# Logits of two of five blocks formed in four column ranges, from bfloat16 pieces

## The chip, the cores and the metric

The kernel runs on one core of one Trainium2 chip. The metric is the time of one execution on the device in microseconds (us). Three runs of the kernel before took 920.73, 920.84 and 923.83 us; their median is 920.84 us.

## The reference, cut to what matters

Three layers follow each other: a linear attention with random features, a gated feed-forward layer, and a layer of eight experts whose routing is greedy and global. The change touches the second layer's hidden rows `h` and the logits of the third.

```python
# x: (2304, 512), from the attention
xn = x / rms * rms_g
g = xn @ w_gate                      # (2304, 1536)
val = xn @ w_val
h = g * (1.0 / (1.0 + np.exp(-g))) * val
y = h @ w_out                        # (2304, 512)
logits = y @ w_gate2                 # (2304, 8)
# tokens are given to experts by the sorted logits, 288 to each of the 8
for e in range(8):
    out[mask_e] = np.maximum(y[mask_e] @ w1[e], 0.0) @ w2[e]
```

The routing orders all 2304 x 8 logits against each other, so the logits need more accuracy than one pass of short numbers gives.

## The kernel before, in words

**Blocks and half-steps.** The 2304 tokens are cut into five blocks `j` = 0 to 4, four of 512 tokens and a last one of 256 (`WIDTH`). The 1536 hidden features are cut into twelve slices `f` of 128. A half-step `(j, f, v)` is the gate product (`v` = 0) or the value product (`v` = 1) of one slice of one block: `ffn_pe` (L652) issues 12 matmuls into a PSUM tile `gv`: four times L659 and L660 (high and low part of the weights against the high part `xh` of the tokens), then four times L662 (high weights, low part `xl`). Every operand is float32r, split into a high and a low part. `ffn_el` (L665) works on the result: for `v` = 0 a tanh on ACT (L671) and a product on DVE (L672), for `v` = 1 the product with the gate on DVE (L684), the high part on ACT (L686), the low part on POOL (L687) and a store of both to DRAM (`h_dr`, L688).

**Logits.** Since `logits = h @ (w_out @ w_gate2)`, they are formed from `h` directly: `wog` holds, for each slice, the 8 columns of `w_out @ w_gate2` as a high and a low part, 16 columns in all. `ffn_lg` (L691) multiplies them with the high part (L698) and the low part (L699) of one slice of one block: two float32r matmuls of 16 weight columns and as many moving columns as the block has tokens, summed over the 12 slices in a PSUM tile `lg`. `ffn_rank` (L705) transposes the sums (L710), adds the halves (L712, L713) and `ranks` (L97 to L101) counts within each token.

**Block 0 comes late.** When block 0 runs, `wog` isn't ready. Its `h` is stored unsplit (L680, L682), and behind the attention a loop reads it back slice by slice (`late_load`, L894), splits it (`late_split`: L899 on ACT, L900 on POOL), writes the parts to DRAM (L901) and forms its logits in a PSUM tile `late`.

**Stages.** From 0 to about 390 us the attention runs in ticks, with half-steps of the blocks between its matmuls. Then comes the loop that begins at `late_load(0)`: 45 half-steps, the rest of block 3 and all of block 4. It is called the tail here. From about 500 us `w_out` is applied to all tokens (`ffn2`, L972) as filler between the matmuls of the routing (`route`; its counting products are L181), and from about 685 us the experts run.

**What sets the order.** In the ticks and in the routing the order of TensorE (PE) is the order in which the code is written. In the tail of the kernel before, a scheduler orders every engine, PE too; on the other engines it may also move work of the tail in front of work of the ticks. Each engine, and the queue of SP that issues nearly all DMAs, works strictly in its order. Tiles come from pools with a fixed number of buffers: `gv` has 2, `ht` 6 (`HB`), `ws` 3 (pool `stage`), `dw` 3, `hp` 2, `th` 2. `wo_split` (L871) loads two slices of `w_out` and splits them, on ACT (L876) and DVE (L877).

Of the kernel before, what the change touches and what calls it, by code (L numbers as in the profile page):

```python
# [9 lines left out]
F32 = mybir.dt.float32  # L10
F32R = mybir.dt.float32r
# [3 lines left out]
OP = mybir.AluOpType  # L15
# [88 lines left out]
def route(nc, keep, sb, ps, cst, L, R, ids, slot, aside, room):  # L104
# [10 lines left out]
    for n in (NSL, SL, 2 * NSL):  # L115
# [176 lines left out]
def kernel(ctx, tc, qT, kT, kC, v1, vC, om, wgv, rms, wo, woT, wg2, w1, w2, cfd, trd, cid, out, dbg=None):  # L292
# [356 lines left out]


    fq, fst, lgs, rks = [], {}, [], []

    def ffn_pe(j, f, v):
        n = WIDTH[j]
        pg = psG.tile([128, BLK], F32, name="gv")
        w = wsl[f].rearrange("p l (v k m) -> p l v k m", k=KD, v=2)
        xh, xl = xblk[j]
        for k in range(KD):
            nc.tensor.matmul(pg[:, :n], w[:, 0, v, k], xh[:, k, :n], start=(k == 0), stop=False)  # L659
            nc.tensor.matmul(pg[:, :n], w[:, 1, v, k], xh[:, k, :n], start=False, stop=False)  # L660
        for k in range(KD):
            nc.tensor.matmul(pg[:, :n], w[:, 0, v, k], xl[:, k, :n], start=False, stop=(k == KD - 1))  # L662
        return pg[:, :n]

    def ffn_el(j, f, v, pg):  # L665
        n = WIDTH[j]
        nh = n // HB2
# [21 lines left out]
        fq.append((j, f, hp))  # L689

    def ffn_lg(j, f, hp):  # L691
        n = WIDTH[j]
        nh = n // HB2
        if f == 0:
            st["lg", j] = (psL if j else psB).tile([2 * E, BLK], F32, name="lg" if j else "late", bufs=1)
        wv = wog[:, f].rearrange("p a e -> p (a e)")
        lg = st["lg", j][:, :n].rearrange("p (b t) -> p b t", b=nh)
        nc.tensor.matmul(lg, wv, hp[:, :nh, 0], start=(f == 0), stop=False)  # L698
        nc.tensor.matmul(lg, wv, hp[:, :nh, 1], start=False, stop=(f == KF - 1))  # L699
        if f == KF - 1:  # L700
# [24 lines left out]
    def ffn_step_pe():  # L725
# [116 lines left out]
    with tc.manual_schedule(engines={mybir.EngineType.PE}):  # L842
# [16 lines left out]
    st["rank"] = lambda: psB.tile([128, 512], F32, name="num", bufs=1)[:, :BLK // 128 * 2 * E].rearrange(  # L859
        "p (c e) -> p c e", e=2 * E)  # L860
# [28 lines left out]
    lates, step = [], 0  # L889

    def late_load(f):
        hs = f2.tile([128, 4, 2, 128], F32R, name="ht", bufs=HB)
        hs = hs.rearrange("p a l t -> p (a l t)").rearrange("p (b l t) -> p b l t", b=BLK // HB2, l=2)
        nc.sync.dma_start(hs.bitcast(F32)[:, :, 1], h_dr[:BLK // HB2, :, f, :HB2].rearrange("b p x -> p b x"))  # L894
        lates.append(hs)

    def late_split(f):
        hs = lates[f]
        nc.scalar.copy(hs[:, :, 0], hs.bitcast(F32)[:, :, 1])  # L899
        nc.gpsimd.tensor_sub(hs[:, :, 1], hs.bitcast(F32)[:, :, 1], hs[:, :, 0])  # L900
        nc.sync.dma_start(h_dr[:BLK // HB2, :, f].rearrange("b p x -> p b x"),  # L901
                          hs.bitcast(F32).rearrange("p b l t -> p b (l t)"))

    late_load(0)
    while True:
        if not ffn_step_pe():
            break
        lf, lv = divmod(step, 2)
        if not lv and 0 < lf <= KF:
            ffn_lg(0, lf - 1, lates[lf - 1])  # L910
        j, f, v = ffn_step_el()
        if lv and lf < KF:
            late_split(lf)
            if lf + 1 < KF:
                late_load(lf + 1)
        if j == NB - 1 and v:
            if f % 2 and f > 1:
                wo_split((f - 3) // 2)
            if f > 6:
                ffn2_load(*seq2[f - 7])  # L920
        step += 1
# [296 lines left out]
```

## Time and profile before

| | |
|---|---|
| median of three runs | 920.84 us |
| the profiled execution, its own time | 922.03 us |
| its span in the trace | 920.2 us |
| granted clock of PE, mean | 0.995 of full speed |
| PE / DVE / ACT / POOL busy | 901.9 / 554.2 / 372.8 / 229.8 us |

The span is the time between the first and the last instruction of the trace; 1.8 us of the execution lie around it. A matmul's row lasts from its start to its modelled end, and matmuls overlap, so the pace of PE is read from the distance between two starts.

### The profile page before, as it was taken

Reading aid. Unit: us, or ns where it says so; the run is one execution under the profiler, and the core shown is the slowest. Engines: PE = TensorE matmul, PEld = TensorE weight load, DVE = VectorE, ACT = ScalarE, POOL = GpSimd, SP = SyncE. Lnnn points to the kernel's source line nnn. Section 1 sums busy time; section 2 is a strip of 40 time slices with the busy share of each in tenths; the row PEclk is TensorE's granted clock in tenths of the full one; section 3 lists DMA queues with packets and bytes.
Section 4 is the critical chain, followed back from the end, with each engine's and each line's share of the span. In section 5 each row is a group of like instructions: output and inputs, shape, how many; then the busy total and the mean of one; then the engine's idle time right before and its main releaser. Section 6 shows DMA issues by size and latency. Waiting matters only on the chain.

```text
span 920.2 us, 16173 instructions
## 1 busy us (share of the span) xinstructions
PE 901.9 (98%) x6171; PEld 783.3 (85%) x6171; DVE 554.2 (60%) x1262; ACT 372.8 (41%) x843; POOL 229.8 (25%) x298
## 2 busy tenths in 40 slices
PE   8998999999999999999999999999999999999996
PEld 7887888888888888877799777777779999999995
DVE  4798896565676775332273666666654655556661
ACT  5985565435554445333252001000014454544541
POOL 1355352122233332275232000000012222122111
PEclk9999999999999999999999999999999999999998
DMA  8556354444345552187564776776623666665550
GB/s 295 182 160 213 120 168 127 135 152 144 115 153 178 184 185 90 69 278 277 189 225 152 202 207 191 211 206 201 171 78 115 193 188 193 189 208 193 184 161 26
DMA packets 113213, 158.88 MB, mean 173 GB/s; under 512 B 6640, under 2 KB 70768, under 8 KB 113136
## 3 DMA queue, kind: packets, MB, share of 16 engines
q1 hardware_dynamic: 107328, 143.57, 49.4%
q0 software_dynamic: 3072, 9.44, 3.4%
q10 hardware_dynamic: 2736, 4.85, 1.4%
q8 instruction: 48, 0.79, 0.3%
q14 instruction: 29, 0.24, 0.1%
HBM read 113.79 MB, written 44.04 MB: 172 GB/s over the span
## 4 chain that ended last, share of the span: by engine, by line
PE 84%; issue 7%; DVE 5%; POOL 2%; DMA 2%; ACT 1%; SPq 0%; POOLq 0%; ACTq 0%; DVEq 0%
PE py L972 16%; PE gv L659 10%; PE gv L660 10%; PE gv L662 10%; PE pm L497 3%; PE ph L1086 3%; PE ph L1083 3%; PE ph L1084 3%; PE py L1094 3%; PE py L1095 3%; PE py L1096 3%; PE pm L440 2%; PE cnt L181 2%; PE pm L486 2%; PE pp L388 1%
## 5 line engine op out<-in xcount | busy, mean ns | idle before, releaser
L659 PE MATMUL gv<-xh,wc 128*128 128x512 f32 (+1 forms) x480 | 180.9, 383 | 2.5 <-DVE th L672 1.9
L660 PE MATMUL gv<-xh,wc 128*128 128x512 f32 (+1 forms) x480 | 175.3, 372 | 0.0
L972 PE MATMUL py<-wc,ht 128*128 128x512 f32 x648 | 167.1, 404 | 0.0
L972 PEld LDWEIGHTS py<-wc,ht 128*128 128x128 f32 x648 | 114.9, 189 | 19.0
L662 PE MATMUL gv<-xl,wc 128*128 128x512 f32 (+1 forms) x480 | 118.4, 369 | 0.0
L659 PEld LDWEIGHTS gv<-xh,wc 128*128 128x128 f32 x480 | 91.1, 190 | 19.5 <-DVE th L672 3.0
L660 PEld LDWEIGHTS gv<-xh,wc 128*128 128x128 f32 x480 | 91.2, 190 | 13.9
L662 PEld LDWEIGHTS gv<-xl,wc 128*128 128x128 f32 x480 | 85.5, 189 | 15.9
L400 ACT ACTIVATE ft<-pp,mx 128x128 f32<-128x128 f32 x288 | 82.3, 372 | 18.5 <-DVE mx L397 16.0
L687 POOL TENSOR_TENSOR hp<-th,hp 128x512 fp32r<-128x512 f32 (+1 forms) x48 | 60.6, 1262 | 114.5 <-ACT hp L686 102.6
L672 DVE SCALAR_TENSOR_TENSOR th<-th,gv 128x512 f32<-128x512 f32 (+1 forms) x60 | 37.9, 632 | 84.4 <-ACT th L671 84.4
L943 DVE TENSOR_TENSOR wc<-ws,wc 128x512 fp32r<-128x512 f32 x128 | 84.8, 683 | 0.0
L1094 PE MATMUL py<-ehh,wc 128*128 128x288 f32 x256 | 77.7, 304 | 0.0
L1095 PE MATMUL py<-ehl,wc 128*128 128x288 f32 x256 | 75.9, 297 | 0.0
L1096 PE MATMUL py<-ehh,wc 128*128 128x288 f32 x256 | 75.8, 296 | 0.0
L1083 PE MATMUL ph<-exh,wc 128*128 128x288 f32 x256 | 71.6, 302 | 0.0
L1084 PE MATMUL ph<-exh,wc 128*128 128x288 f32 x256 | 69.8, 295 | 0.0
L983 ACT COPY ys<-py 128x512 f32<-128x512 f32 x18 | 10.6, 587 | 144.6 <-PE py L972 103.7
L953 ACT CAST wc<-ws 128x1024 fp32r<-128x1024 f32 x64 | 66.9, 1046 | 2.7 <-ACT ys L983 2.4
L397 DVE TENSOR_REDUCE mx<-pp 128x4 f32<-128x512 f32 (+1 forms) x76 | 50.0, 657 | 16.6 <-PE pp L393 10.1
L1088 DVE SCALAR_TENSOR_TENSOR ehl<-ph,ehh 128x288 fp32r<-128x288 f32 x64 | 29.3, 458 | 46.8 <-ACT ehh L1087 46.8
L671 ACT ACTIVATE th<-gv 128x512 f32<-128x512 f32 (+1 forms) x60 | 33.2, 554 | 59.4 <-PE gv L662 52.0
(214 smaller groups left out, 1717.5 us busy)
## 6 DMA issues: line engine op xcount, KB each, us to landing
ws<-in_w_dram SPq DMA_DIRECT2D x64, 512.0 KB, 4.3
ht<-h_dr SPq DMA_DIRECT2D x54, 512.0 KB, 4.1
h_dr<-hp SPq DMA_DIRECT2D x36, 512.0 KB, 2.9
ws<-in_wgv_dram SPq DMA_DIRECT2D x24, 512.0 KB, 4.3
h_dr<-hp SPq DMA_DIRECT2D x24, 256.0 KB, 2.3
ws<-in_woT_dram SPq DMA_DIRECT2D x12, 512.0 KB, 3.6
ws<-in_wo_dram SPq DMA_DIRECT2D x12, 512.0 KB, 3.7
h_dr<-ht SPq DMA_DIRECT2D x12, 512.0 KB, 3.1
```

Source lines behind the costliest of these rows:

```text
L400: nc.scalar.activation(ft[:n, g], pp[:n, g], AF.Exp, bias=mx[:n, g:g + 1])
L659: nc.tensor.matmul(pg[:, :n], w[:, 0, v, k], xh[:, k, :n], start=(k == 0), stop=False)
L660: nc.tensor.matmul(pg[:, :n], w[:, 1, v, k], xh[:, k, :n], start=False, stop=False)
L662: nc.tensor.matmul(pg[:, :n], w[:, 0, v, k], xl[:, k, :n], start=False, stop=(k == KD - 1))
L943: nc.vector.tensor_sub(w[:, 1, h], sv[:, h], w[:, 0, h])
L953: nc.scalar.copy(w[:, 0], sv)
L972: nc.tensor.matmul(py, ht[:, i4, a], w[:, l, f % 2], start=(f == 0 and n == 0), stop=(f == KF - 1 and n == 2))
L1083: nc.tensor.matmul(ph, w[:, 0, k, m], xh[:, k], start=(k == 0), stop=False)
L1084: nc.tensor.matmul(ph, w[:, 1, k, m], xh[:, k], start=False, stop=False)
L1094: nc.tensor.matmul(py, w[:, 0, k], hh[:, k], start=(k == 0), stop=False)
L1095: nc.tensor.matmul(py, w[:, 0, k], hl[:, k], start=False, stop=False)
L1096: nc.tensor.matmul(py, w[:, 1, k], hh[:, k], start=False, stop=(k == KE - 1))
```

## The change

The logits of block 0 and block 3 (the first and the fourth) are formed in another way.

- The weights `wog` are added up to float32 and cut into three bfloat16 pieces: 24 columns of a slice, padded with zeros to 32 (`wb`, in the room of the later tile `ge6`).
- `h` of these blocks is cut into three bfloat16 pieces as well (`split3`: two subtractions on DVE). A piece is the upper or lower half of a float32 word, and is read with a stride of two.
- `group` takes four slices at a time: for each of the three pieces four matmuls, whose outputs lie in partitions 0 to 31, 32 to 63, 64 to 95 and 96 to 127 of a PSUM tile. A slice's place among the four turns from group to group. The sums of both blocks are transposed whole, 128 x 128, and one reduction on DVE adds the 16 parts of each logit.
- The tail's loop is written out anew (`tail`), and PE follows its code. PSUM tiles of half-steps alternate in pairs between `gv` and `py`, two buffers each. The stored rows of block 0 are loaded four ahead. A group stands three half-steps or more behind the half-step that gave its last piece. Loads of `w_out` stand a step ahead of their splits.
- `late_split` writes the high and low part from two `dw` tiles in two DMAs, where one DMA wrote both from `ht`.

```diff
-        nc.vector.scalar_tensor_tensor(th, pg, 0.5, th, op0=OP.mult, op1=OP.mult)
-        h = th.rearrange("p (b t) -> p b t", b=nh)
+        pc = st["pieces"]() if "pieces" in st and j in WIDE else None
+        hs = pc[:, 0] if pc is not None else th
+        nc.vector.scalar_tensor_tensor(hs, pg, 0.5, th, op0=OP.mult, op1=OP.mult)
+        h = hs.rearrange("p (b t) -> p b t", b=nh)
...
+    def split3(pc):
+        h, r = pc[:, 0], pc[:, 1]
+        nc.vector.tensor_sub(r, h, half(h, 1))
+        nc.vector.tensor_sub(half(r, 0), r, half(r, 1))
+
+    def group(four):
+        for n in range(3):
+            for i, (j, f, pc) in enumerate(four):
+                if ("lg", j) not in st:
+                    st["lg", j] = (psL if j else psB).tile([128, BLK], F32, name="lg" if j else "late", bufs=1)
+                src = (half(pc[:, 0], 1), half(pc[:, 1], 1), half(pc[:, 1], 0))[n]
+                nc.tensor.matmul(st["lg", j][32 * i:32 * i + 32, :WIDTH[j]], st["wb"][:, f], src,
+                                 start=(j, i) not in begun, stop=n == 2, skip_group_check=True)
+                begun.add((j, i))
+        for j, f, _ in four:
+            if f == KF - 1:
+                ls = fp.tile([128, BLK], F32, name="th")
+                nc.scalar.copy(ls[:, :WIDTH[j]], st.pop(("lg", j))[:, :WIDTH[j]])
+                wide.append((j, ls))
...
+        for j, ls in wide[:1]:
+            n, c = WIDTH[j] // 128, j * BLK // 128
+            pl = st["rank"]()
+            for i in range(n):
+                nc.tensor.transpose(pl[:, i, :], ls[:, i * 128:(i + 1) * 128], ident)
+            nc.vector.tensor_reduce(out=L[:, c:c + n, :], in_=pl[:, :n].rearrange("p c (g e) -> p c e g", e=E),
+                                    axis=AX.X, op=OP.add)
...
+    def tail():
...
+        step, born, gone, turns, nsplit = 0, [], 0, 0, 0
+        while ffn_step_pe(*(("gv", psG), ("py", psB))[step // 2 % 2]):
+            if step > 2 and born[step - 3] - gone >= 4:
+                four = [pq.pop(0) for _ in range(4)]
+                group(four[turns:] + four[:turns])
+                gone, turns = gone + 4, (turns + 1) % 4
+            j, f, v = ffn_step_el()
+            if v and j in WIDE:
+                split3(pq[-1][2])
+            if nsplit < KF and (step % 2 == 0 or step == 1):
+                late_split(nsplit)
+                nsplit += 1
+            elif step % 2 and len(lates) < KF:
+                late_load(len(lates))
+            if j == NB - 1 and v:
+                if f % 2:
+                    if f > 1:
+                        wo_split((f - 3) // 2)
+                    wo_load(f // 2)
...
     def late_load(f):
-        hs = f2.tile([128, 4, 2, 128], F32R, name="ht", bufs=HB)
...
+        pc = room4() if f % 3 == 2 else stage.tile([128, 2, BLK], F32, name="ws")
...
     def late_split(f):
...
+        pc = lates[f]
+        hi, lo = (fp.tile([128, DM], F32, name="dw", bufs=DW) for _ in range(2))
+        nc.scalar.copy(hi.bitcast(F32R), pc[:, 0])
+        nc.gpsimd.tensor_sub(lo.bitcast(F32R), pc[:, 0], hi.bitcast(F32R))
+        for n, w in enumerate((hi, lo)):
+            nc.sync.dma_start(h_dr[:BLK // HB2, :, f, n * HB2:(n + 1) * HB2].rearrange("b p x -> p b x"),
+                              w.rearrange("p (b x) -> p b x", x=HB2))
+        split3(pc)
+        pq.append((0, f, pc))
...
-        if not lv and 0 < lf <= KF:
-            ffn_lg(0, lf - 1, lates[lf - 1])
...
+    for f in range(4):
+        late_load(f)
+    st["pieces"] = room4
+    with tc.manual_schedule(engines={mybir.EngineType.PE}):
+        tail()
```

PE, first logits of both blocks in the tail (`lg` is block 3, `late` block 0). Before, one slice of each block follows a value product:

```order
L662 MATMUL gv<-xl,wc 128x512 x4
L698 MATMUL lg<-hp,wog 16x512
L699 MATMUL lg<-hp,wog 16x512
L698 MATMUL late<-ht,wog 16x512
L699 MATMUL late<-ht,wog 16x512
L659 MATMUL gv<-xh,wc 128x512
```

Now the first group stands there: two slices of block 3 and two of block 0, in the column ranges 0 to 3.

```order
L666 MATMUL gv_4475<-xl_3174,wc_501 128x512 x4
L714 LDWEIGHTS ge6_4353
L714 MATMUL lg_4488<-ht_4371,ge6_4353 32x512
L714 LDWEIGHTS ge6_4353
L714 MATMUL lg_4488<-ht_4389,ge6_4353 32x512
L714 LDWEIGHTS ge6_4353
L714 MATMUL late_4491<-ws_4361,ge6_4353 32x512
L714 LDWEIGHTS ge6_4353
L714 MATMUL late_4491<-ws_4363,ge6_4353 32x512
L714 LDWEIGHTS ge6_4353
L714 MATMUL lg_4488<-ht_4371,ge6_4353 32x512
```

The last row begins the second of three such sets of four. There are six groups, 72 matmuls, behind half-steps 4, 7, 11, 15, 19 and 23 of the tail; the 48 matmuls L698 and L699 of the two blocks are gone, and those of block 4 stay.

ACT, where block 4 begins (the rows with 128x256 are block 4). Before:

```order
L671 ACTIVATE th<-gv 128x256
L876 CAST wc<-ws 128x1024
L686 CAST hp<-th 128x256
L702 COPY th<-lg 16x512
L671 ACTIVATE th<-gv 128x256
L712 COPY lt<-num 128x32
L876 CAST wc<-ws 128x1024
L686 CAST hp<-th 128x256
L702 COPY th<-late 16x512
```

Now (L675, L692, L720 and L920 are L671, L686, L702 and L876 of before):

```order
L675 ACTIVATE th<-gv 128x256
L920 CAST wc<-ws 128x1024
L692 CAST hp<-th 128x256
L720 COPY th<-lg 128x512
L720 COPY th<-late 128x512
L920 CAST wc<-ws 128x1024
L675 ACTIVATE th<-py 128x256
L675 ACTIVATE th<-gv 128x256
L692 CAST hp<-th 128x256
```

Both copies of sums and a cast of `w_out` now stand in front of the second gate of block 4 (`th<-py`), whose matmuls come before the last group.

SP's queue in the last ticks of the attention (`wo_dr<-dw` is the last of the conversions of `w_out`). Before:

```order
L621 DMA wo_dr<-dw 128x512
L873 DMA ws<-wo_dr 128x2x512
L688 DMA h_dr<-hp 128x2x512
L621 DMA wo_dr<-dw 128x512
L873 DMA ws<-wo_dr 128x2x512
L688 DMA h_dr<-hp 128x2x512
```

Now:

```order
L625 DMA wo_dr<-dw 128x512
L973 DMA ws<-h_dr 128x2x256
L694 DMA h_dr<-hp 128x2x512
L983 DMA h_dr<-dw 128x2x256
L625 DMA wo_dr<-dw 128x512
L973 DMA ws<-h_dr 128x2x256
L694 DMA h_dr<-hp 128x2x512
L983 DMA h_dr<-dw 128x2x256 x3
L625 DMA wo_dr<-dw 128x512
```

The first two slices of block 0 are read back, split and written within the ticks, where three loads of `w_out` stood. Their splits on ACT and POOL stand there too.

## Rows read from the trace of the kernel before

**Rows 1.** The page: busy time, share, instructions; then the chain that ended last.
```profile
PE 901.9 (98%) x6171; PEld 783.3 (85%) x6171; DVE 554.2 (60%) x1262; ACT 372.8 (41%) x843; POOL 229.8 (25%) x298
PE 84%; issue 7%; DVE 5%; POOL 2%; DMA 2%; ACT 1%; SPq 0%; POOLq 0%; ACTq 0%; DVEq 0%
```

**Rows 2.** Busy us by stretch: PE, PEld, DVE, ACT, POOL; clock, DMA share, GB/s.
```profile
393.00:461.00 68.00, 68.00 (x303) 51.96 (x302) 17.74 (x29) 19.74 (x35) 32.51 (x31) 1.00 0.71 247
461.00:500.00 39.00, 39.00 (x320) 37.10 (x319) 21.91 (x51) 16.20 (x34) 14.18 (x14) 1.00 0.62 208
500.00:685.00 185.00, 183.93 (x1559) 138.63 (x1557) 120.71 (x418) 18.33 (x29) 3.72 (x4) 1.00 0.64 184
```

**Rows 3.** Instructions of block 0's sums: ns min/median/max, first and last start.
```profile
L698 PE MATMUL late<-ht,wog x12: 389/396/397, 402.9 to 468.1; 128*16 128x512 f32 x12
L699 PE MATMUL late<-ht,wog x12: 389/391/397, 403.1 to 468.3; 128*16 128x512 f32 x12
```

**Rows 4.** Timeline, first logits of the tail: start us, us, engine, instruction.
```profile
402.42 0.39 PE L698 MATMUL lg<-hp,wog 128*16 128x512 f32 x1
...
403.11 0.40 PE L699 MATMUL late<-ht,wog 128*16 128x512 f32 x1
403.34 0.39 PE L659 MATMUL gv<-xh,wc 128*128 128x512 f32 x1
```

**Rows 5.** Timeline, a counting product of the routing between filler.
```profile
508.78 2.77 PE L972 MATMUL py<-wc,ht 128*128 128x512 f32 x11
511.40 0.61 PE L181 MATMUL cnt<-oh,ge 128*128 128x8 bf16 x18
511.86 0.71 PE L972 MATMUL py<-wc,ht 128*128 128x512 f32 x2
```

**Rows 6.** Timeline, transposes of 128 columns and of 16.
```profile
380.41 0.60 PE L502 MATMUL pm<-cf,xn 128*128 128x128 f32 x4
...
393.27 0.42 PE L710 MATMUL lg<-cf,th 16*128 16x16 f32 x4
```

**Rows 7.** Groups by line, 461 to 500 us: count, busy us, mean ns, idle before.
```profile
L687 POOL TENSOR_TENSOR hp<-th,hp 128x256 fp32r<-128x256 f32 x11 | 12.4, 1125 | 23.3 <-ACT hp L686 23.3
L877 DVE TENSOR_TENSOR wc<-ws,wc 128x1024 fp32r<-128x1024 f32 x6 | 7.3, 1221 | 1.6 <-ACT wc L876 1.6
L876 ACT CAST wc<-ws 128x1024 fp32r<-128x1024 f32 x6 | 6.3, 1050 | 6.2 <-PE gv L662 6.2
L672 DVE SCALAR_TENSOR_TENSOR th<-th,gv 128x256 f32<-128x256 f32 x12 | 5.0, 418 | 11.8 <-ACT th L671 11.8
L684 DVE SCALAR_TENSOR_TENSOR th<-gv,th 128x256 f32<-128x256 f32 x11 | 4.6, 422 | 3.7 <-PE gv L662 3.7
L671 ACT ACTIVATE th<-gv 128x256 f32<-128x256 f32 x12 | 4.6, 384 | 8.7 <-POOL hp L687 5.0 <-PE gv L662 3.6
L686 ACT CAST hp<-th 128x256 fp32r<-128x256 f32 x11 | 4.4, 402 | 7.3 <-DVE th L684 5.8 <-DMA h_dr<-hp 1.5
...
L702 ACT COPY th<-late 16x512 f32<-16x512 f32 x1 | 0.6, 571 | 0.0
```

**Rows 8.** Timeline, a gate product of block 4 and the value product behind it.
```profile
494.23 0.28 PE L659 MATMUL gv<-xh,wc 128*128 128x256 f32 x1
...
495.67 0.28 PE L659 MATMUL gv<-xh,wc 128*128 128x256 f32 x1
```

**Rows 9.** Timeline, start of the tail: a gate's product on DVE, a later half-step.
```profile
394.28 0.69 DVE L672 SCALAR_TENSOR_TENSOR th<-th,gv 128x512 f32<-128x512 f32 x1 [2.31 <-ACT th L671]
...
396.95 0.39 PE L659 MATMUL gv<-xh,wc 128*128 128x512 f32 x1
```

**Rows 10.** Timeline, last ticks: a split on POOL, its use on PE.
```profile
347.66 0.86 POOL L384 TENSOR_TENSOR kl<-qt,kh 128x256 fp32r<-128x256 f32 x1 [4.28 <-PE pm L502]
...
353.62 0.28 PE L390 MATMUL pp<-omh,kl 128*128 128x256 f32 x1
```

**Rows 11.** Timeline, stores of block 4 in SP's queue, with their wait.
```profile
489.77 6.45 SPq L688 DMA_DIRECT2D h_dr<-hp  x3
```

More of the change, by code (lines that the diff above doesn't have):

```diff
@@ L56 @@
 LATE = 2
+GE6 = (NC - 1) * 63 + 128
+WIDE = (0, NB - 2)
 C_ID, C_SL, C_SA, C_C, C_P, C_E, C_T, C_N = 0, 128, 224, 248, 266, 267, 275, 339
@@ L119, in route @@
     ges = {5: room[:, off:off + (NC - 1) * 31 + 128],
-           6: sb.tile([128, (NC - 1) * 63 + 128], BF, name="ge6", bufs=1)}
+           6: sb.tile([128, GE6], BF, name="ge6", bufs=1)}
     for g in ges.values():
@@ L651, with ffn_pe @@
     fq, fst, lgs, rks = [], {}, [], []
-    def ffn_pe(j, f, v):
+    pq, wide, begun = [], [], set()
+    def ffn_pe(j, f, v, pg):
         n = WIDTH[j]
-        pg = psG.tile([128, BLK], F32, name="gv")
         w = wsl[f].rearrange("p l (v k m) -> p l v k m", k=KD, v=2)
@@ L688, in ffn_el, with half @@
         nc.sync.dma_start(dst, hf[:, :nh].rearrange("p b l t -> p b (l t)"))
-        fq.append((j, f, hp))
+        if pc is None:
+            fq.append((j, f, hp))
+        else:
+            pq.append((j, f, pc))
+    def half(t, i):
+        return t.bitcast(BF).rearrange("p (t w) -> p t w", w=2)[:, :, i]
+    def split3(pc):
[16 more added lines that the diff above has]
+                wide.append((j, ls))
     def ffn_lg(j, f, hp):
@@ L694, in ffn_lg @@
         if f == 0:
-            st["lg", j] = (psL if j else psB).tile([2 * E, BLK], F32, name="lg" if j else "late", bufs=1)
+            st["lg", j] = psL.tile([128, BLK], F32, name="lg", bufs=1)[:2 * E]
         wv = wog[:, f].rearrange("p a e -> p (a e)")
@@ L709, in ffn_rank @@
             for i in range(n):
-                nc.tensor.transpose(pl[:, i, :], ls[:, i * 128:(i + 1) * 128], ident[:2 * E, :2 * E])
+                nc.tensor.transpose(pl[:, i, :2 * E], ls[:, i * 128:(i + 1) * 128], ident[:2 * E, :2 * E])
             lt = fp.tile([128, BLK // 128, E], F32, name="lt")
-            nc.scalar.copy(lt[:, :n], pl[:, :n, E:])
+            nc.scalar.copy(lt[:, :n], pl[:, :n, E:2 * E])
             nc.vector.tensor_add(L[:, c:c + n, :], pl[:, :n, :E], lt[:, :n])
@@ L715, in ffn_rank @@
         lgs.clear()
+        for j, ls in wide[:1]:
[5 more added lines that the diff above has]
+                                    axis=AX.X, op=OP.add)
+            rks.extend(range(c, c + n, 2))
+        del wide[:1]
     st["eng"] = nc.gpsimd
@@ L723, in ffn_rank_el, with ffn_step_pe @@
         rks.clear()
-    def ffn_step_pe():
+    def ffn_step_pe(name="gv", pool=psG):
         if not ready or ready[0][1:] not in gvs or (fq and fq[0][1] not in wogs):
@@ L728, in ffn_step_pe @@
         j, f, v = ready.pop(0)
-        pg = ffn_pe(j, f, v)
+        pg = ffn_pe(j, f, v, pool.tile([128, BLK], F32, name=name))
         if (f, v) == (KF - 1, 1):
@@ L858 @@
     st["eng"] = nc.vector
-    st["rank"] = lambda: psB.tile([128, 512], F32, name="num", bufs=1)[:, :BLK // 128 * 2 * E].rearrange(
-        "p (c e) -> p c e", e=2 * E)
+    st["rank"] = lambda: psB.tile([128, 512], F32, name="num", bufs=1).rearrange("p (c e) -> p c e", e=128)
     ci = rp.tile([128, cid.shape[1]], I32, name="ci", bufs=1)
@@ L869, with wo_load, wo_split @@
     wos, hts = [], {}
-    def wo_split(c):
+    def wo_load(c):
         sv = stage.tile([128, 2, DM], F32, name="ws")
         nc.sync.dma_start(sv, wo_dr[2 * c:2 * c + 2].rearrange("f p d -> p f d"))
+        wos.append(sv)
+    def wo_split(c):
+        sv = wos[c]
         w = wpool.tile([128, 2, 1024], F32R, name="wc")
@@ L877, in wo_split @@
         nc.vector.tensor_sub(w[:, 1], sv, w[:, 0])
-        wos.append(w)
+        wos[c] = w
     def ffn2_load(c, g):
@@ L888, with room4 @@
     seq2 = [(c, g) for c in order for g in range(3)]
-    lates, step = [], 0
+    lates, grown = [], {}
+    def room4():
+        ht = f2.tile([128, 4, 2, 128], F32R, name="ht", bufs=HB)
+        return ht.bitcast(F32).rearrange("p f l t -> p (f l t)").rearrange("p (a t) -> p a t", a=2)
+    def tail():
+        for j, f, hp in fq:
+            pc = room4()
+            nc.vector.tensor_add(pc[:, 0].rearrange("p (b t) -> p b t", t=HB2), hp[:, :, 0], hp[:, :, 1])
+            split3(pc)
+            pq.append((j, f, pc))
+        fq.clear()
+        step, born, gone, turns, nsplit = 0, [], 0, 0, 0
[17 more added lines that the diff above has]
+                    wo_load(f // 2)
+                if f > 6:
+                    ffn2_load(*seq2[f - 7])
+            born.append(gone + len(pq))
+            step += 1
+        assert step > 2 * KF and not pq
@@ L891, in late_load @@
     def late_load(f):
-        hs = f2.tile([128, 4, 2, 128], F32R, name="ht", bufs=HB)
-        hs = hs.rearrange("p a l t -> p (a l t)").rearrange("p (b l t) -> p b l t", b=BLK // HB2, l=2)
-        nc.sync.dma_start(hs.bitcast(F32)[:, :, 1], h_dr[:BLK // HB2, :, f, :HB2].rearrange("b p x -> p b x"))
-        lates.append(hs)
+        pc = room4() if f % 3 == 2 else stage.tile([128, 2, BLK], F32, name="ws")
+        nc.sync.dma_start(pc[:, 0].rearrange("p (b x) -> p b x", x=HB2),
+                          h_dr[:BLK // HB2, :, f, :HB2].rearrange("b p x -> p b x"))
@@ L897, in late_split @@
+        lates.append(pc)
     def late_split(f):
[L898 to L908, printed above, removed]
-        if not lv and 0 < lf <= KF:
-            ffn_lg(0, lf - 1, lates[lf - 1])
[L911 to L921, printed above, removed]
@@ L922 @@
-    assert step > 2 * KF
+        pc = lates[f]
[5 more added lines that the diff above has]
+                              w.rearrange("p (b x) -> p b x", x=HB2))
+        split3(pc)
+        pq.append((0, f, pc))
@@ new lines @@
+    wb = rp.tile([128, GE6], BF, name="ge6", bufs=1)[:, :KF * 32].rearrange("p (f e) -> p f e", e=32)
+    wt = room4().rearrange("p a t -> p (a t)")[:, :KF * 2 * E].rearrange("p (f a e) -> p f a e", a=2, e=E)
+    st["wb"] = wb
+    nc.vector.memset(wb, 0.0)
+    nc.vector.tensor_add(wt[:, :, 0], wog[:, :, 0], wog[:, :, 1])
+    nc.vector.tensor_copy(wb[:, :, :E], wt[:, :, 0])
+    nc.vector.tensor_sub(wt[:, :, 1], wt[:, :, 0], wb[:, :, :E])
+    nc.vector.tensor_copy(wb[:, :, E:2 * E], wt[:, :, 1])
@@ L923 @@
+    nc.vector.tensor_sub(wb[:, :, 2 * E:3 * E], wt[:, :, 1], wb[:, :, E:2 * E])
+    for f in range(4):
[3 more added lines that the diff above has]
+        tail()
     wo_split(KF // 2 - 1)
```

## The prediction

> **What bounds the kernel now.** I read the page's busy shares and its chain first. PE is busy for 901.9 of 920.2 us and holds 84% of the chain [rows 1]. So the question for each edit is whether it takes time from PE or adds a wait to it. Next come the stretches. The tail (393 to 500 us) and the routing behind it show PE busy all the time at the full clock of 2.4 GHz, while DVE, ACT and POOL are busy for 18, 20 and 33 of 68 us, and then for 22, 16 and 14 of 39 us [rows 2]. A busy row does not show how fast PE goes, since rows overlap. The timeline does: in the tail a matmul with 512 columns starts every 0.23 us, whatever its weights. From 402.42 to 403.34 us, four logit matmuls with 16 weight columns take 0.92 us [rows 4], as long as four with 128 would. No gap stands ahead of them or behind. The routing that follows fills its waits with `ffn2`, and PE is busy for 183.93 of 185 us there [rows 2], so what the tail saves or loses reaches the end.
>
> **The change part by part.**
>
> *Removed.* Blocks 0 and 3 have 12 slices each and two matmuls per slice: 48 matmuls, all in the tail (those of `late` run from 402.9 to 468.1 us [rows 3]). 48 x 0.23 = 11.0 us of PE.
>
> *Added.* Six groups of 12 matmuls with 512 columns. No row of before shows two matmuls in different column ranges, so the bounds come from the nearest rows. If the four of a set run one after the other, a group takes 12 x 0.23 = 2.76 us, and with 0.1 us to enter 2.9 us. If they run fully side by side it takes 3 x 0.23 = 0.7 us. The nearest row for issue is the counting product, which is bfloat16 with its weight loads apart, as a group is: 18 pairs take 511.86 - 511.40 = 0.46 us, so 0.026 us a pair. Entering it from float32r costs 511.40 - 508.78 - 11 x 0.23 = 0.1 us, and leaving costs nothing that can be seen [rows 5]. These pairs start 0.026 us apart while a single one lasts far longer, so PE does hold several products at once. I take the end at which the ranges work beside each other, since the four outputs share no column, and add the issue of the other three: 3 x (0.23 + 3 x 0.026) + 0.1 = 1.02 us. Six groups take 6.1 us. Difference so far: -4.9 us.
>
> The Trainium skill prices this in "TensorE: Matmul & The Clock Gate", Part 3: three column tiles ran 2.38 times as fast as one after the other. An estimate from that, at the same efficiency, is 0.29 us for a set of four and 0.97 us for a group, which would make the difference -5.2 us; no row here shows it.
>
> *Transposes.* Eight transposes of 16 columns become eight of 128. Four of the one last 0.42 us, four of the other 0.60 us, ends included [rows 6]. What follows both starts without a gap, so I take 0; the bounds are 0 and 0.4 us.
>
> *More work on other engines.* 24 slices need two subtractions each. The nearest DVE row with 512 columns lasts 0.69 us [rows 9], so 48 of them are 33 us, in a stretch where DVE is idle for 50 of 68 us [rows 2]. This is hidden because a group stands three half-steps (about 8 us) behind its last piece, and the `gv`/`py` tiles now give DVE and ACT four buffers in place of two. Without that cover each late piece would stop PE for its 1.4 us.
>
> *Into the ticks.* The scheduler puts the reading back and the splits of two slices in front of the end of the attention. On POOL that is two subtractions, 2 x 1.3 us, ahead of a split that now runs at 347.66 us behind 4.28 us of idle time, and which PE needs at 353.62 us [rows 10]. The idle time and 5 us of slack hide them: 0, at worst 1 us.
>
> *Start of the tail.* Preparing `wb` and the first pieces puts six small DVE instructions and three of 0.69 us ahead of the gate's product that runs at 394.28 us. The half-step that needs its buffer starts at 396.95 us, or 0.46 us earlier without the two logit matmuls ahead of it [rows 4, 9]. About 0.8 us of slack is left if they run back to back behind the preceding instructions. I take 0.3 us, with bounds 0 and 1.
>
> *Start of block 4.* This is the wait that I expect to see. On ACT, the second gate of block 4 now stands behind both copies of sums and a cast of `w_out`. After the last group ends at T: two copies 1.14, cast 1.05, gate 0.38, so T + 2.6. On DVE the subtraction of `w_out` that waits for that cast stands ahead of the gate's product: 2.2 + 1.22 = T + 3.4, the product 0.42, a small ranking instruction 0.3, the value's product 0.42, so T + 4.55. ACT's cast 0.40 makes T + 5.0 and POOL's part 0.7 to 1.8 (mean 1.1) makes T + 6.1 [rows 7]. PE wants it after three half-steps of 1.44 us [rows 8], a pair of logit matmuls and two transposes: 4.3 + 0.24 + 0.7 = T + 5.2. It waits for about 0.9 us, and behind it stands all of PE's work; I take 1.0 us, with bounds 0 and 4 (below).
>
> *Sum.* -11.0 + 6.1 + 0 + 0 + 0.3 + 1.0 = -3.6 us. The profiled execution took 922.03 us, so its like would take 918.4 us; from the median of 920.84 us the forecast is **917.2 us**. With all bounds on one side, a saving of 6.9 us; on the other, a loss of 12 us.
>
> **The rivals.**
>
> *The four ranges run one after the other.* Then six groups cost 6 x 2.9 = 17.4 us, and the sum is -11.0 + 17.4 + 1.3 = +7.7 us: 928.5 us. For it: in rows 4 narrow weights are no cheaper than wide ones, and nothing in the trace of before shows two at once over 512 columns. Against it: the four stand in ranges of their own, which those of rows 4 did not, and rows 5 show quick issue. It decides from 1.6 us a group on, where the gain is gone; from 2.4 us a group on the kernel is slower by over 0.5%.
>
> *The waits at block 4 take the gain.* SP's queue is in order: in block 4 stores already hold it for 6.45 us in one stretch [rows 11]. In the changed kernel loads of `w_out` and of rows for `ffn2` come in a bunch there. If a store lands some 3 us later, ACT's next cast, whose buffer it frees, is late by as much, and the logits behind it on PE too: waits of 4 to 5 us in place of 1.3, and 920.9 us. Against it: block 4 has ACT and DVE idle for more than 40% of its time [rows 2].
>
> *Each group drains PE.* A last matmul lasts 0.39 us though the next starts after 0.23 us [rows 4], so an emptied array costs 0.16 us, and a weight load that nothing covers costs 0.19 us more (mean of PEld rows in this stretch, 51.96 us over 302 with narrow ones included: 0.17 us [rows 2]). At entry and exit of six groups that is 12 x 0.35 = 4.2 us, and the time is 921.4 us. Against it: going into and out of the narrow matmuls and the bfloat16 ones costs 0 to 0.1 us now [rows 4, 5]. The Trainium skill states the rule in "TensorEngine Tiling (Array Packing)", Key Properties: changing the tiling mode drains the engine; the trace of before shows no such gap, but has no product outside the first range.
>
> *Nothing waits.* No waits and groups of 0.7 to 0.85 us: a saving of 6 to 6.9 us, 914.4 us.
>
> **How the numbers follow.** What a measurement of this kernel can tell from no change is about 0.5%, 4.6 us: below 916.2 it is faster, above 925.4 slower. Chances: the forecast 0.40 (its own range 915 to 919.5, a quarter of it faster); nothing waits 0.14, faster; waits take the gain 0.17, same; draining 0.13, same, with a little on the slow side; one after the other 0.16, slower. So faster 0.10 + 0.14 = 0.24; same 0.30 + 0.17 + 0.11 = 0.58; slower 0.16 + 0.02 = 0.18. The range leaves out half of the case below and a bit of the one above: 914.2 to 928.6 us.
>
> **What would show it.** In the profile after, each group should take about 1.0 us from the start of its first matmul to the start of the next half-step: about 0.3 us a set, with starts a few hundredths apart, shows the ranges side by side; 0.23 us between all twelve shows them one after the other; a hole ahead of and behind each group shows draining. DVE should be busy for about 33 us more in the tail, without PE waiting for a piece. The logits of block 4's second slice should wait for ACT or POOL for about 1 us. `ffn2` should start some 3.6 us earlier than now. I am wrong if a group takes over 1.6 us, if PE waits inside the ticks, or if the waits of block 4 sum to over 4 us.

## The result, and the profile after

The changed kernel takes 927.43 us (median of seven runs, 925.16 to 929.94), the kernel before 921.2 us (seven runs, 920.73 to 923.84). The ratio is 1.0058, with a 95% interval from 1.0039 to 1.0077. The forecast was 917.2 us: the time moved the other way, by 0.6%. The profiled execution took 926.7 us, 4.7 us more than that of before.

The page of the changed kernel, the row that answers to the first of [rows 1]:

```profile
PE 899.0 (97%) x6195; PEld 781.0 (84%) x6195; DVE 599.1 (65%) x1317; ACT 372.1 (40%) x841; POOL 235.2 (25%) x298
```

PE has 2.9 us less to do, and the span is 4.7 us longer: PE waits, or goes slower. The first two stretches of [rows 2], with the same columns, say where:

```profile
393.00:461.00 68.00, 64.83 (x312) 49.09 (x313) 55.77 (x70) 17.48 (x32) 32.42 (x26) 0.97 0.57 194
461.00:500.00 39.00, 35.49 (x288) 33.63 (x287) 23.94 (x53) 15.69 (x30) 15.19 (x16) 0.96 0.88 280
```

Before, PE was busy for all of the first two stretches at the full clock. Now it is idle for 3.2 and 3.5 us of them, and the mean clock is 0.97 and 0.96. DVE's 17.7 us have become 55.8 in the first. In the third stretch PE is busy for 184.70 of 185 us, as before. To compare executions I take the tail from the last small transposes of block 2 to the first weights of `ffn2`. Before, it lasts from 393.5 us (the last of the four that start at 393.27 in [rows 6]) to 500.3 us, 106.8 us:

```profile
L972 PEld LDWEIGHTS py<-wc,ht x648: 187/188/201, 500.3 to 683.3; 128*128 128x128 f32 x162
```

In the changed kernel it lasts from 392.8 to 505.2 us:

```profile
L742 PE MATMUL lg<-cf,th x8: 208/208/230, 293.0 to 392.8; 16*128 16x16 f32 x8
...
L1052 PEld LDWEIGHTS py<-wc,ht x648: 187/188/201, 505.2 to 688.2; 128*128 128x128 f32 x162
```

That is 112.4 us, 5.6 more. The first group, in the timeline of PE (it answers to [rows 4]):

```profile
405.97 1.07 PE L666 MATMUL gv<-xl,wc 128*128 128x512 f32 x4
406.97 0.40 PE L714 MATMUL lg<-ht,ge 128*32 128x512 bf16 x2
406.97 0.40 PE L714 MATMUL late<-ws,ge 128*32 128x512 bf16 x2
407.21 0.39 PE L714 MATMUL lg<-ht,ge 128*32 128x512 bf16 x2
...
407.76 0.50 PE L663 MATMUL gv<-xh,wc 128*128 128x512 f32 x1
408.10 0.39 PE L664 MATMUL gv<-xh,wc 128*128 128x512 f32 x1
```

Four matmuls start together and the next four 0.24 us later. Entering costs 0.09 us, the three sets 0.79, and the first matmul behind them holds the next back by 0.11 (0.34 in place of 0.23): 1.0 us, as forecast. So the loss lies elsewhere. What PE waited for from 393 to 510 us (engine, tile and line, releaser: us in total, times, longest):

```profile
PE lg L714 <- DVE ht L706: 3.2, 2, 2.4
PE lg L730 <- ACT hp L692: 1.9, 1, 1.9
PE lg L731 <- POOL hp L693: 1.8, 3, 1.0
```

In the tail of before there was one wait, of 0.2 us, ahead of logits of block 4:

```profile
PE lg L699 <- POOL hp L687: 0.2, 1, 0.2
```

The longest wait of the changed kernel, in the timeline of all engines:

```profile
438.55 0.69 DVE L705 TENSOR_TENSOR ws<-ws 128x512 f32<-128x512 f32 x1 [1.75 <-DMA ws<-h_dr]
...
439.16 0.68 DVE L705 TENSOR_TENSOR ht<-ht 128x512 f32<-128x512 f32 x1
439.28 1.71 POOL L981 TENSOR_TENSOR dw<-ws,dw 128x512 fp32r<-128x512 f32 x1 [4.45 <-ACT dw L980]
439.76 1.82 DVE L706 TENSOR_TENSOR ws<-ws 128x512 bf16<-128x512 f32 x1
...
440.95 1.71 POOL L693 TENSOR_TENSOR hp<-ht,hp 128x512 fp32r<-128x512 f32 x1
441.48 1.77 DVE L706 TENSOR_TENSOR ht<-ht 128x512 bf16<-128x512 f32 x1
...
443.30 0.48 PE L714 MATMUL lg<-ht,ge 128*32 128x512 bf16 x1 [2.44 <-DVE ht L706]
```

DVE's second subtractions (L706) last 1.8 us where one alone lasts 0.75, and GpSimd's 1.71 where one alone lasts 1.29. They take turns: each that starts while the other engine's is running ends 0.6 us (DVE) or 1.1 to 1.2 us (GpSimd) behind the end of that one. Two such delays are 2.1 of the 2.44 us for which the last matmul of the fourth group waits.

Rows of DVE and GpSimd that start within 0.02 us of each other show that the second to start is the one that lasts longer:

```profile
405.79 1.29 POOL L693 TENSOR_TENSOR hp<-ht,hp 128x512 fp32r<-128x512 f32 x1 [3.52 <-ACT hp L692]
405.81 1.89 DVE L706 TENSOR_TENSOR ht<-ht 128x512 bf16<-128x512 f32 x1
...
460.96 0.76 DVE L706 TENSOR_TENSOR ht<-ht 128x512 bf16<-128x512 f32 x1
460.98 1.86 POOL L693 TENSOR_TENSOR hp<-ht,hp 128x512 fp32r<-128x512 f32 x1 [3.77 <-ACT hp L692]
461.60 0.68 DVE L676 SCALAR_TENSOR_TENSOR th<-th,py 128x512 f32<-128x512 f32 x1
```

The last row has one operand in PSUM (`py`) and runs wholly beside GpSimd's subtraction, and keeps its length: over the whole trace the products L676 and L690, each with one operand in PSUM, last at most 0.692 us. Over the tail, DVE's groups by line (count | busy us, mean ns):

```profile
L706 DVE TENSOR_TENSOR ht<-ht 128x512 bf16<-128x512 f32 x16 | 17.4, 1085 | 0.3
L705 DVE TENSOR_TENSOR ht<-ht 128x512 f32<-128x512 f32 x16 | 14.1, 880 | 2.7 <-DMA ht<-h_dr 2.4
...
L706 DVE TENSOR_TENSOR ws<-ws 128x512 bf16<-128x512 f32 x5 | 7.1, 1437 | 0.0
L705 DVE TENSOR_TENSOR ws<-ws 128x512 f32<-128x512 f32 x5 | 4.4, 906 | 8.1 <-DMA ws<-h_dr 8.1
```

These 42 subtractions (the other six of the 48 stand in the ticks) take 43.0 us; undisturbed they would take 30 (e6 has 30.2). A hole, a stretch in which PE stands still, can also cost something behind it. The stretches of the hole, behind it, and of the hole at block 4 and behind that:

```profile
440.40:443.30 2.90, 0.46 (x11) 0.00 (x0) 2.90 (x3) 0.00 (x0) 2.27 (x2) 1.00 0.42 142
443.40:446.90 3.50, 3.50 (x9) 2.51 (x9) 3.11 (x5) 1.12 (x2) 1.48 (x1) 0.51 0.38 150
...
471.80:473.90 2.10, 0.18 (x3) 0.02 (x1) 1.61 (x5) 0.40 (x1) 0.00 (x0) 1.00 1.08 371
474.00:477.50 3.50, 2.93 (x15) 2.76 (x14) 1.23 (x1) 1.35 (x2) 1.60 (x2) 0.52 1.10 340
```

In the 3.5 us behind the two holes, of 2.44 and 1.92 us, the granted clock is 0.51 and 0.52, the level of 1.2 GHz. Behind the first hole six matmuls in a row start 0.43 us after the one before in place of 0.23, and with those around them 1.5 us are lost; behind the second it is 1.2 us.

At block 4, the store of block 3's last slice is issued behind loads as soon as its low part is done, takes long to land, and the cast that needs its buffer follows when it has landed. Timeline of SP and ACT, then the store's time to landing (issues from 464 to 470 us):

```profile
463.79 1.98 SPq L928 DMA_DIRECT2D ht<-h_dr  x2
465.87 2.71 SPq L694 DMA_DIRECT2D h_dr<-hp  x2
...
473.43 0.40 ACT L692 CAST hp<-th 128x256 fp32r<-128x256 f32 x1 [2.41 <-DVE rk_q L103]
```

```profile
DMA to landing us min/median/max: 7.5/7.5/7.5
```

465.9 + 7.5 = 473.4 us, and the cast starts at 473.43. (The row names the last event on DVE instead.) The DMA engines are busy all the time there: the DMA share is 1.08 in the stretch of the hole, and 0.88 from 461 to 500 us, where it was 0.62 [rows 2].

### The profile page after: what moved, and what is told of

It is laid out like the page before. It is cut to its first block, busy times and chain, and to the rows that moved or that the text cites. A ratio compares the mean times of both kernels' runs of the same rounds, so it can differ in the third digit from the quotient of the medians.

```text
span 924.9 us, 16323 instructions
## 1 busy us (share of the span) xinstructions
PE 899.0 (97%) x6195; PEld 781.0 (84%) x6195; DVE 599.1 (65%) x1317; ACT 372.1 (40%) x841; POOL 235.2 (25%) x298
## 4 chain that ended last, share of the span: by engine, by line
PE 78%; issue 8%; DVE 5%; POOL 3%; DMA 3%; ACT 2%; SPq 0%; POOLq 0%; ACTq 0%; DVEq 0%
PE py L1052 16%; PE gv L663 8%; PE gv L664 8%; PE gv L666 8%; PE pm L501 3%; PE ph L1166 3%; PE ph L1163 3%; PE ph L1164 3%; PE py L1174 3%; PE py L1175 3%; PE py L1176 3%; PE pm L444 2%; PE cnt L185 2%; PE pm L490 2%; DMA ws<-in_wgv_dram 1%
## 5 line engine op out<-in xcount | busy, mean ns | idle before, releaser
L663 PE MATMUL gv<-xh,wc 128*128 128x512 f32 (+1 forms) x392 | 154.0, 397 | 3.2 <-DVE th L676 2.6
L664 PE MATMUL gv<-xh,wc 128*128 128x512 f32 (+1 forms) x392 | 147.5, 380 | 0.0
L666 PE MATMUL gv<-xl,wc 128*128 128x512 f32 (+1 forms) x392 | 100.0, 377 | 0.0
L663 PEld LDWEIGHTS gv<-xh,wc 128*128 128x128 f32 x392 | 74.6, 190 | 22.7 <-issue 4.9
L664 PEld LDWEIGHTS gv<-xh,wc 128*128 128x128 f32 x392 | 74.5, 190 | 12.1
L666 PEld LDWEIGHTS gv<-xl,wc 128*128 128x128 f32 x392 | 71.2, 188 | 14.3
L693 POOL TENSOR_TENSOR hp<-th,hp 128x512 fp32r<-128x512 f32 (+1 forms) x37 | 44.8, 1212 | 90.9 <-ACT hp L692 84.5
L676 DVE SCALAR_TENSOR_TENSOR th<-th,gv 128x512 f32<-128x512 f32 (+1 forms) x49 | 31.8, 649 | 37.6 <-ACT th L675 37.6
L575 ACT ACTIVATE dw<-ws 128x512 f32<-128x512 f32 x48 | 32.4, 678 | 50.9 <-DMA ws<-in_wo_dram 22.8
```

## The experiments

Each ratio is against runs of the kernel before on the same chip. "Tail" is the stretch defined above, "groups" and "block 4" are PE's waits there, from the profiled execution. They leave out waits at the start of the tail (1.3 us in e3, 0.4 in e5, 1.0 in e10) and ahead of the transposes of the sums (1.1 us in e4, 0.3 in e10).

| | median us | ratio, 95% interval | tail | groups | block 4 |
|---|---|---|---|---|---|
| before | 921.2 | 1 | 106.8 | - | 0.2 |
| changed | 927.43 | 1.0058 [1.0039, 1.0077] | 112.4 | 3.2 | 3.7 |
| e1 three buffers | 928.27 | 1.0074 [1.0047, 1.0101] | 112.7 | 5.0 | 3.1 |
| e2 DVE in code order | 927.53 | 1.0054 [1.0033, 1.0075] | 112.2 | 2.2 | 4.5 |
| e3 low parts zeroed | 919.62 | 0.9973 [0.9958, 0.9987] | 104.4 | 0 | 1.4 |
| e4 ranges in turn | 930.44 | 1.0082 [1.0061, 1.0104] | 112.9 | 3.3 | 2.9 |
| e5 copies on GpSimd | 920.0 | 0.9966 [0.9954, 0.9978] | 103.3 | 0 | 1.2 |
| e6 low parts on ACT | 919.27 | 0.9961 [0.9948, 0.9975] | 103.2 | 0 | 1.5 |
| e7 e6 and e1 | 918.64 | 0.9947 [0.9928, 0.9966] | 102.8 | 0 | 0.9 |
| e8 preparation later | 918.16 | 0.9942 [0.9924, 0.996] | 103.1 | 0 | 1.7 |
| e9 one range | 929.41 | 1.0076 [1.0059, 1.0093] | 114.3 | 0 | 0.7 |
| e10 changed again | 929.23 | 1.0088 [1.0066, 1.0111] | 114.8 | 3.5 | 3.8 |

**e1.**

```diff
-        hp = fp.tile([128, BLK // HB2, 2, HB2], F32R, name="hp")
+        if "pieces" in st and j == NB - 1:
+            hp = fp.tile([128, 1, 2, HB2], F32R, name="dw", bufs=DW)
+        else: ...
```

> The two parts of block 4's rows stand in three `dw` tiles (free by then) in place of two `hp` tiles; all else as in the changed kernel. Theory (a late store): in the changed kernel the cast of block 4's second slice runs at 473.43 us because the store that must free its `hp` tile is issued at 465.9 us and lands 7.5 us later, among bunched loads. With a third tile the cast follows its product: the waits of 1.9 and 0.6 us on PE ahead of that slice's logits shrink to the 0.9 us or less that the order on ACT and DVE gives, and the 1.2 us that PE loses at the low clock behind them goes too: 2.5 to 3.7 us less, 924 to 925 us. Rival (the order on ACT and DVE sets the wait): the cast still comes at T + 6 to 8 us, T being the end of the last group, and the time stays at 927 us.

The wait ahead of the second slice shrank from 1.9 + 0.6 to 0.5 us, so its cause was the late store:

```profile
476.39 0.29 PE L734 MATMUL lg<-dw,wog 128*16 128x256 f32 x1 [0.47 <-POOL dw L696]
```

The time did not follow: waits on GpSimd came in later slices and the groups waited longer. DVE, ACT and GpSimd work in the same order as in the changed kernel, but behind the hole of 2.91 us in the fourth group the granted clock stayed at 1.00 here. PE reached the fifth group earlier and waited 2.1 us there in place of 0.7, and the clock fell to 0.5 behind that one. PE's waits:

```profile
PE lg L717 <- DVE ht L709: 4.2, 2, 2.9
PE lg L734 <- POOL dw L696: 3.1, 5, 1.2
```

**e2.**

```diff
-    with tc.manual_schedule(engines={mybir.EngineType.PE}):
+    with tc.manual_schedule(engines={mybir.EngineType.PE, mybir.EngineType.DVE}):
         tail()
```

> DVE too follows the code in the tail, as PE does; the subtractions of a block 3 slice stand directly behind its product and ahead of those of block 0's slice that was read back. Theory (DVE's order): the wait of 2.4 us in the fourth group comes from a block 3 slice whose product was done at 436.8 us and whose subtractions stand behind those of a slice that landed at 438.5 us; in code order they are done by 438.5 us, the group does not wait, and the 1.5 us lost at the low clock behind it go too: about 4 us less, 923 us. Rival (the late rows themselves): the read-back slice holds DVE as long as before, now in front of the next gate's product, so that a gate waits in place of a group: 926 to 930 us.

The rival's time. The fourth and fifth groups don't wait, but the third does for 0.4 us and the sixth for 1.7 us, behind this subtraction, which stands beside one of GpSimd (462.32 to 464.16 us); and block 4 waits longer. Timeline of DVE:

```profile
462.97 1.74 DVE L705 TENSOR_TENSOR ht<-ht 128x512 f32<-128x512 f32 x1
```

Another order only chooses which piece is held up.

**e3.**

```diff
-        nc.gpsimd.tensor_sub(hp[:, :nh, 1], h, hp[:, :nh, 0])
+        if pc is None: ...
+        else:
+            nc.gpsimd.memset(hf[:, :nh, 1], 0.0)
-        nc.gpsimd.tensor_sub(lo.bitcast(F32R), pc[:, 0], hi.bitcast(F32R))
+        nc.gpsimd.memset(lo, 0.0)
```

> Leaves out the low parts of blocks 0 and 3 in the tail: GpSimd writes zeros in place of its subtraction, so that it reads nothing while DVE cuts pieces. Theory (DVE and GpSimd hold each other up): every subtraction of the pieces then lasts 0.69 to 0.77 us where 15 or so of 42 last 1.4 to 1.9 us now; DVE is busy for about 15 us less in the tail; the fourth group waits for at most 0.4 us and the fifth for nothing, so 5 us less with the clock: 922 us. Rival (the late rows): the holes are those of the rows that land late, the subtractions get shorter but the waits of 2.4 and 0.7 us stay above 1.5 us together: 926 us.

As the theory said, and somewhat more. No group waits, and the subtractions have their own length though GpSimd writes beside them:

```profile
L709 DVE TENSOR_TENSOR ht<-ht 128x512 bf16<-128x512 f32 x16 | 12.3, 770 | 0.4
L708 DVE TENSOR_TENSOR ht<-ht 128x512 f32<-128x512 f32 x16 | 11.0, 688 | 0.5 <-DMA ht<-h_dr 0.3
```

The late rows of block 0 alone hold no group up. But GpSimd also had less to do here (0.53 us a fill), so e5 and e6.

**e4.**

```diff
-        for n in range(3):
-            for i, (j, f, pc) in enumerate(four):
+        for i, (j, f, pc) in enumerate(four):
+            for n in range(3):
```

> In a group the three pieces of one column range follow each other, then the next range's, instead of one matmul in each range in turn. Theory (a range is busy for 0.23 us, and PE starts matmuls in the order of the code): only the last of one range and the first of the next start together, nine starts 0.23 us apart, so a group costs 2.1 to 2.3 us in place of the 1.02 us that the undisturbed groups of the changed kernel cost: 6 x 1.2 = 7 us more, 934 us. Rival (PE looks past a busy range): the groups keep 1.0 us, and the time stays at 927 us.

My theory fell. The three of a range follow each other in the program, and still all four ranges start together, so PE does not start matmuls of different ranges strictly in the order of the program:

```profile
410.58 0.41 PE L714 MATMUL lg<-ht,ge 128*32 128x512 bf16 x2
410.60 0.42 PE L714 MATMUL late<-ws,ge 128*32 128x512 bf16 x2
```

A group that nothing holds up costs 1.03 to 1.06 us. The median is above the changed kernel's, but the tail is not longer (112.9 to 112.4); the intervals of the two ratios overlap, and the profiled execution entered the tail 3.6 us later, ahead of the part that e4 edits.

**e5.**

```diff
-        nc.gpsimd.tensor_sub(lo.bitcast(F32R), pc[:, 0], hi.bitcast(F32R))
+        nc.gpsimd.tensor_copy(lo.bitcast(F32R), pc[:, 0])
```

(and as much for `hp`)

> Leaves out the subtraction that gives the low parts of blocks 0 and 3 in the tail: GpSimd copies the row instead, so it reads one operand where the changed kernel reads two and e3 none. Theory (any read of GpSimd holds DVE's second operand up): DVE's subtractions of the pieces still last 1.2 us or more where a copy runs beside them, in 8 or more of 42; the groups wait for about 1 to 3 us in all; 922 to 926 us. Rival (what e3 gained was GpSimd's shorter work and the earlier stores, or only two operands hold DVE up): all subtractions last 0.69 to 0.77 us, no group waits, and the time is e3's 919.6 us.

Half of each: the subtractions go as the theory said, though none lasts 1.2 us, and the time is the rival's. One operand read by GpSimd is enough to hold DVE up; but the copy is short, so the delay is 0.3 to 0.4 us in place of 1.1, and the three half-steps of slack hold it. By line (ns min/median/max):

```profile
L709 DVE TENSOR_TENSOR ht<-ht x16: 740/1048/1057, 397.0 to 459.8; 128x512 bf16<-128x512 f32 x16
```

**e6.**

```diff
...
+        else:
+            split3(pc)
+            nc.scalar.copy(hp[:, :nh, 0], half(pc[:, 0], 1)...)
+            nc.scalar.copy(hp[:, :nh, 1], pc[:, 1]...)
...
-            if v and j in WIDE:
-                split3(pq[-1][2])
...
-        nc.scalar.copy(hi.bitcast(F32R), pc[:, 0])
-        nc.gpsimd.tensor_sub(lo.bitcast(F32R), pc[:, 0], hi.bitcast(F32R))
+        split3(pc)
+        nc.scalar.copy(hi.bitcast(F32R), half(pc[:, 0], 1))
+        nc.scalar.copy(lo.bitcast(F32R), pc[:, 1])
...
-        split3(pc)
```

> The whole computation, with the high part cut instead of rounded: the high part is the upper half of the row, the low part ACT's cast of the difference that DVE forms for the pieces anyway, so GpSimd has no work for blocks 0 and 3 in the tail. Theory (DVE and GpSimd hold each other up): as in e3 the subtractions last 0.69 to 0.77 us, the groups don't wait, and the tail from the last small transposes to the first product with `w_out` takes 104 to 106 us in place of the 112.4 us of the changed kernel: 919 to 921 us. Rival (e3 gained by less work in all): 22 more casts of 0.62 us on ACT, 14 us, come ahead of tanh and stores; block 4 waits for 3 to 4 us as in the changed kernel and a gate waits in front of it: 923 to 926 us.

The theory's numbers, with the whole computation and more work on ACT. Subtractions by line over the tail, then the first stretch of [rows 2]:

```profile
L711 DVE TENSOR_TENSOR ht<-ht 128x512 bf16<-128x512 f32 x16 | 12.1, 755 | 0.3
L710 DVE TENSOR_TENSOR ht<-ht 128x512 f32<-128x512 f32 x16 | 11.1, 691 | 2.2 <-DMA ht<-h_dr 2.0
```

```profile
393.00:461.00 68.00, 68.00 (x354) 52.94 (x353) 46.36 (x78) 31.43 (x56) 4.75 (x11) 1.00 0.69 229
```

DVE's busy time falls from 55.8 to 46.4 us, ACT's rises from 17.5 to 31.4, and PE is busy throughout.

**e7** is e6 with the edit of e1.

> e6 with block 4's parts in three `dw` tiles as in e1. Theory (late stores set block 4's waits, as e1's second slice showed: 0.5 us in place of 2.5): 1 to 2 us less than e6, 917.5 to 919.5 us. Rival (GpSimd's own order sets them): the waits of the second halves on GpSimd, 1.4 us in e3, stay, and the time is e6's.

Block 4's waits fall to 0.9 us and the tail to 102.8 us. The gain over e6, 0.4 us in the tail, is below what the timed runs tell apart.

**e8.**

```diff
+            if step == 1:
+                prep()
+                for n, (a, b, hp) in enumerate(first): ...
...
```

> e7 with the preparation of `wb` and of the first pieces written behind the second half-step of the tail in place of ahead of the first. Theory (DVE's work ahead of the tail's first gate product delays it, 1.3 us in e3): that wait goes, 1 us less than e7, 916.5 to 918.5 us. Rival (DVE's work only moves): the first group, three half-steps on, waits for its pieces for 1 us or more, and the time is e7's or above.

Inconclusive: neither e6 nor e7 had the wait that it was to remove, the first group doesn't wait, and the time is e7's. Both e7 and e8 beat the kernel before by 0.5%, with intervals below 1.

**e9.**

```diff
-                nc.tensor.matmul(st["lg", j][32 * i:32 * i + 32, :WIDTH[j]], ...
+                nc.tensor.matmul(st["lg", j][:32, :WIDTH[j]], ...
...
```

> e7 with all four matmuls of a set in the first column range, summed there; the other 96 rows of the sums are zeros. Theory (matmuls overlap because they stand in ranges of their own): the twelve of a group start 0.23 us apart, a group costs 2.8 to 2.9 us in place of 1.0, so the tail is 6 x 1.85 = 11 us longer and the time is 929 to 930 us. Rival (narrow bfloat16 matmuls overlap wherever they stand): the groups keep 1.0 us and the time is e7's 918.6 us.

```profile
408.55 0.62 PE L722 MATMUL lg<-ht,ge 128*32 128x512 bf16 x2
409.02 0.61 PE L722 MATMUL late<-ws,ge 128*32 128x512 bf16 x2
...
411.36 0.50 PE L663 MATMUL gv<-xh,wc 128*128 128x512 f32 x1
```

Twelve starts 0.23 us apart: a group costs 3.0 us, and the tail is 11.5 us longer than e7's. It is the range, not the narrowness, that lets matmuls overlap.

**e10** is the changed kernel, unaltered.

> The changed kernel as it is, on the chip of e9. The same holes should show, since the order of every engine is fixed: one of about 2.5 us in the fourth group, one under 1 us in the fifth, 2 to 4 us at block 4; 926 to 929 us, and the tail 112 to 113 us. If the holes came from one execution's chance, they would lie elsewhere or be gone.

The holes are where they were:

```profile
PE lg L714 <- DVE ht L706: 3.5, 2, 2.7
PE lg L730 <- ACT hp L692: 2.1, 1, 2.1
...
PE gv L663 <- DVE th L676: 1.0, 1, 1.0
```

The last row is the wait at the start of the tail that the prediction bounded by 1 us; the first execution had none. It is 1.0 of the 2.4 us by which this tail is longer than that of the first execution; both the tail and the median lie above what I had expected.

## Why the prediction was wrong

**Groups: right.** 1.0 us where nothing held one up (1.01 to 1.04 among 512-column half-steps, as the delay of what follows), against 1.02. e9 priced the rival in which ranges run one after the other: 3.0 us a group against 2.9, 929.41 us against 928.5. That the measured time lies near it is a coincidence of other causes. Draining costs 0.2 us a group at most and is part of the 1.0. The Trainium skill, "TensorEngine Tiling (Array Packing)", Key Properties, says both that switching the mode drains PE and that tiles operate independently; e4 and e9 agree with the second, and for the first the rows have 0.09 us in and 0.11 us out.

**The step that failed: "This is hidden because a group stands three half-steps (about 8 us) behind its last piece".** I priced each subtraction at 0.69 us, from [rows 9], and so at nothing on PE's path. That row has one operand in PSUM; the new ones have both in SBUF, and GpSimd reads SBUF for 21 subtractions of its own in the same stretch. Side by side both last up to 1.9 us. Behind a late row the slack of 8 us was used up: the fourth and fifth groups cost 4.3 and 1.15 us more than 1.02, clock included, 5.5 us in all. e3, e5 and e6 take away or shorten what GpSimd reads, and all 5.5 us are gone. One of the prediction's signs of being wrong came, a group of over 1.6 us: from the first matmul to the next half-step these two take 3.7 and 1.9 us, through their waits and not through the ranges.

The trace of before could have told. There, DVE's conversions with both operands in SBUF and GpSimd's subtractions spread widely (ns min/median/max, by line; the second row holds two shapes, and its 730 belongs to 128x256):

```profile
L576 DVE SCALAR_TENSOR_TENSOR dw<-ws,dw x48: 674/753/1672, 14.2 to 348.2; 128x512 int32<-128x512 int32 x48
```

```profile
L687 POOL TENSOR_TENSOR hp<-th,hp x48: 730/1288/1812, 175.5 to 501.4; 128x512 fp32r<-128x512 f32 x36, 128x256 fp32r<-128x256 f32 x12
```

I read a mean of 1125 ns for 128x256 in [rows 7] and didn't ask why a shape that takes 730 at best averages that. The products with one operand in PSUM, L672 and L684, have no such spread: none lasts over 0.692 us. The Trainium skill says it in "SBUF — State Buffer", Who interferes with whom: a DVE instruction with two SBUF inputs contends with a GpSimd instruction that reads SBUF, not with one that only writes, and the second to start waits for the first. The rows agree: means of 0.69 and 0.77 us beside fills (e3), mostly 1.05 beside copies (e5), up to 1.9 beside subtractions, and of two that start together the second is the longer (405.79 and 460.96 us).

**Block 4: mechanism named, size wrong.** Forecast 1.0 us; 3.7 us of waits and 1.2 us at the low clock came. For the second slice (1.9 and 0.6 us) it is the second rival, the late store, as e1 showed; the other 1.2 us are waits for GpSimd's low parts. The waits also fell to 1.5 us in e6, and to 0.9 us in e7, near the forecast: how much of the fall in e6 is due to earlier stores and how much to other work of GpSimd is open.

**The clock: left out.** No term had a price for PE's speed after a wait. Behind two holes of about 2 us another 2.7 us were lost at 1.2 GHz.

**The rest: right.** No wait in the last ticks, nothing to see at the transposes, 0 and 1.0 us at the start of the tail in the two executions (forecast 0.3, bounds 0 and 1).

**The sum.** -11.0 + 6.1 + 5.5 + 4.9 = +5.5 us, against 5.6 us by which the tail grew. (The prediction's bounds, all on the side of a loss, add up to 12.8 us and not 12; nothing hangs on it.) In e6, where GpSimd has no work for blocks 0 and 3, the tail is 103.2 us, 3.6 us shorter than before: the forecast's own sum, with 1.5 us of waits at block 4 where it had 1.0, and none at the start of the tail where it had 0.3.

## What to carry to other kernels

Price an added DVE instruction by a row with its operands in the same memories, and look for what GpSimd reads at that time; a wide spread between minimum and maximum at one shape is the sign. Slack behind a piece counts only as far as the longest instruction, in order, that can come in between. A wait of about 2 us on PE cost 1.2 to 1.5 us more at the lower clock behind it in the changed kernel; behind one of 2.91 us in e1 PE kept its pace, so this is a risk to allow for and not a fixed price.

## What the runs showed of the hardware

Matmuls with 32 weight columns in four column ranges overlap fully, 1.0 us for twelve of 512 columns, in both orders of the program that were run (e4 has the other), and not at all in one range (e9). A GpSimd fill that only writes leaves DVE's two-operand subtractions at means of 0.69 and 0.77 us; beside GpSimd subtractions they last up to 1.9 us, while products with one operand in PSUM keep 0.69. A store of 512 KB issued among loads took 7.5 us to land; the median of that line's stores from 440 to 480 us was 3.5.
